# One more bank, regrouped splits and another pace of weight decoding in a fused attention and two-FFN kernel

## The chip, the cores and the metric

The kernel is one program on one core of a Trainium2 chip. The metric is the device time of one execution in microseconds (us). The engines are named as in the profile: PE (TensorE, matrix products), DVE (VectorE), ACT (ScalarE), POOL (GpSimd) and SP (SyncE, which only issues DMAs). Each engine works through its own instructions in order.

## The reference

Attention with a causal window of 128 and a distance bias per head, then two feed-forward layers with different activations. The FFN weights arrive as float64.

```python
scores = scale * np.matmul(q, k.transpose(0, 1, 3, 2))        # 4 x 8 heads, 576 x 576, head_dim 64
scores = np.where((rel >= 0) & (rel < 128), scores + bias[None], -1e9)
attn = exp(scores - max); attn = attn / (sum + 1e-9)
x = np.matmul(attn, v)            # -> (2304 tokens, 512)

h = x @ w_in                      # first FFN: 512 -> 2048
x = (h * np.cos(h)) @ w_out       # 2048 -> 512

h = x @ w_in2                     # second FFN
g = np.where(h >= 1, h, np.where(h <= -1, 0.0, (h + 1) ** 2 / 4))
out = g @ w_out2
```

## The kernel before

**Precision.** Each FFN product is made of three float32r matmuls: an operand is split into a rounded part (hi, by a cast on ACT) and a remainder (lo, by a subtraction on DVE, `sub_lo`), and hi x hi, hi x lo and lo x hi are added up in PSUM. `split_x` does this for the activations (one cast, one subtraction for each of 4 tiles `d`), `split_w2` for the second FFN's weights (its subtraction is on POOL).

**Attention.** 36 pairs (two blocks of 128 queries, two heads) pass through a pipeline written out by hand: in round `k` PE computes the scores of pair k+3 (`pe_s`), the transposes of pair k (`pe_t`, banks h0 and h1) and the products with V of pair k-1 (`pe_v`, banks h2 and h3), while DVE and ACT make scores and exponentials (`scores`), POOL scales by the reciprocal sums (`normalise`), `copy_t` brings the transposes from PSUM to SBUF and `put_x` the results. In the last four rounds (k = 33 to 36) there is no new pair.

**FFNs.** Tokens go through in chunks (`PARTS`). Chunk 0 has two parts, 512 and 256 tokens; chunks 1 to 3 have 512 each; the second FFN has four chunks of 512 and one of 256. A chunk has 16 steps `f` (128 of the 2048 hidden columns each). Per part and step, `mm_a` is 12 matmuls into one PSUM bank (below: an h run), `chain` is the activation function on that bank, and `mm_b` is 12 matmuls that add into the four banks y0 to y3 (a y run). For the first FFN the chain is: ACT scales h to an integer `k` (line 353), DVE takes the fraction (355), ACT takes the Sin (357), DVE multiplies with h (359), ACT casts to `gh` (371), DVE subtracts to `gl` (`sub_lo`, line 80). The chain is a generator: at each of its three yields, other work can be put between.

In chunk 0 the wide part has the one bank h0 and the narrow part h1, since h2 and h3 hold the narrow part's y. PE's order in step f is: wide h run of f, wide y run of f-1, narrow h run of f, narrow y run of f-1. In the other chunks an h run has four banks in turn, and the y run follows two steps later (`LAG`).

**Weight decoding.** `halves` turns float64 weights into float32 with integer operations, half a tile at a time; each `make` issues one DVE instruction of it, with ACT's help (lines 113 and 138). For the first FFN this gives 128 instructions; 17 are issued during attention, the rest in chunk 0 by `slot()`, up to 8 in a step. For the second FFN there are 96, issued in chunks 1 to 3 at the yields of the chains and spread over `KEEP_STEPS` of their 48 steps; their results go to DRAM (`wd`) and are read back in chunk 3 (`stage_f32`), step by step, for `split_w2`, as the first FFN's weights in SBUF are done with. The incoming weights and the reloads share three SBUF tiles (`ld`).

At a chunk's last step `split_x` prepares the next chunk's input; in chunk 0 it stands behind the wide part's chain, in the others one tile is put at each yield of the chain, in place of decoding.

All five engines' instructions are in the order of the program, in one block.

Of the kernel before, what the change touches and what calls it, by code (L numbers as in the profile page):

```python
# [9 lines left out]
F32 = mybir.dt.float32  # L10
# [3 lines left out]
AF = mybir.ActivationFunctionType  # L14
ALU = mybir.AluOpType
ENG = mybir.EngineType
# [7 lines left out]
KD, NF = DM // 128, DFF // 128  # L24
# [2 lines left out]
PARTS = ((((0, 512), (512, 256)), ((768, 512),), ((1280, 512),), ((1792, 512),)),  # L27
         (((0, 512),), ((768, 512),), ((1280, 512),), ((1792, 512),), ((512, 256),)))
LAG = 2
KEEP_STEPS = 42  # L30
N_W1, N_W2 = 8 * NF, 6 * NF
AHEAD = 3

# [1 line left out]
D_FROM = 4  # L35
PT = "DADADADD"
XE = "DA"
ORDERED = {ENG.PE, ENG.DVE, ENG.Activation, ENG.Pool, ENG.SP}


@with_exitstack
def attention_moe_moe_kernel(
# [10 lines left out]
    ACT, DVE, POOL, PE, SP = nc.scalar, nc.vector, nc.gpsimd, nc.tensor, nc.sync  # L53

    one = ctx.enter_context(tc.tile_pool(name="one", bufs=1))
# [8 lines left out]
    chunks = [dict(m=m, parts=parts, last=i == len(PARTS[m]) - 1)  # L64
              for m in range(2) for i, parts in enumerate(PARTS[m])]
# [7 lines left out]
    def small(name, dtype=F32, shape=(128, 512)):  # L73
        return two.tile(list(shape), dtype, tag="s", name=nm(name), bufs=12)
# [82 lines left out]
    made = [0, 0]  # L157
# [90 lines left out]
    def normalise(p):  # L248
        for j in range(2):
            st, sc, w = p["st"], p["sc"][j], p["w"][j]  # L250
            POOL.tensor_tensor(  # L251
                out=sc[:, :, 0:w], in0=sc[:, :, 0:w],
                in1=st[:, 8 + 2 * j:10 + 2 * j].unsqueeze(2).to_broadcast([128, 2, w]), op=ALU.mult)
# [14 lines left out]
    def copy_t(p, j):  # L268
        p["pt"][j] = pt = small("pt")
        n = 2 * p["w"][j]  # L270
        if PT[copies[0] % len(PT)] == "A":
            ACT.copy(pt[:, 0:n], p["tb"][j][:, 0:n])
        else:
            DVE.tensor_copy(pt[:, 0:n], p["tb"][j][:, 0:n])
        copies[0] += 1
# [18 lines left out]
    def put_x(p):  # L294
        t0 = p["b0"] * 128
        o, w = max(a for a in all_parts if a[0] <= t0)
        if (o, p["hp"]) not in x_tiles:
            x_tiles[o, p["hp"]] = new_x(w)
        x = x_tiles[o, p["hp"]][0][:, t0 - o:t0 - o + 256]
        if XE[evicted[0] % len(XE)] == "A":  # L300
            ACT.copy(x, p["vb"][:, 0:256])
        else:
            DVE.tensor_copy(x, p["vb"][:, 0:256])
        evicted[0] += 1


    half = one.tile([128, 1], F32, name="half")
    half_pi = one.tile([128, 1], F32, name="half_pi")

    def free_xs(c, i):  # L310
        for d in range(KD):
            free_x(c["xs", i, d][2])

    def split_x(c, i, ds):
        o, w = c["parts"][i]
        for d in ds:
            x, slot = x_tiles.pop((o, d))
            hi, hi_slot = new_x(w, F32R)
            lo = x_lo(4 * i + d)[:, 0:w]
            ACT.copy(hi, x)  # L320
            sub_lo(DVE, lo, x, hi)
            free_x(slot)
            c["xs", i, d] = hi, lo, hi_slot
# [3 lines left out]
    def mm_a(c, i, f):  # L327
        hi, lo = weights[c["m"], f]
        if len(c["parts"]) > 1:
            tag = f"h{i}"  # L330
        else:
            h_no[0] = (h_no[0] + 1) % 4
            tag = f"h{h_no[0]}"
        w = c["parts"][i][1]
        h = ps.tile([128, 512], F32, tag=tag, name=nm("h"))[:, 0:w]
        n = 0
        for d in range(KD):
            xh, xl, _ = c["xs", i, d]
            s = slice(d * 128, d * 128 + 128)
            for a, x in ((hi, xh), (hi, xl), (lo, xh)):  # L340
                PE.matmul(h, lhsT=a[:, 0, s], rhs=x, start=(n == 0), stop=(n == 11))  # L341
                n += 1
        c["h", i, f] = h
# [64 lines left out]
            if c["m"]:  # L408
                SP.dma_start(out[d * 128:(d + 1) * 128, o:o + w], s)

    def body():
        load(0)
        dist_sb.append(two.tile([128, 512], F32, tag="k", name="dist_sb", bufs=1)[:, 0:256])
        SP.dma_start(dist_sb[0], dist)
        load(1)
        DVE.memset(half, 0.5)
        DVE.memset(half_pi, TWO_PI / 4)
        make_identity(nc, ident)
        np_ = len(pairs)
        c0 = chunks[0]  # L420
        splits = [(i, d) for i in range(len(c0["parts"])) for d in range(KD)]
        for k in range(-AHEAD, np_ + 1):
            new = pairs[k + AHEAD] if k + AHEAD < np_ else None
            mid = pairs[k + AHEAD - 1] if 0 <= k + AHEAD - 1 < np_ else None
            nrm = pairs[k + AHEAD - 2] if 0 <= k + AHEAD - 2 < np_ else None
            cur = pairs[k] if 0 <= k < np_ else None
            old = pairs[k - 1] if k >= 1 else None
            load(k + AHEAD + 1)
            load(k + AHEAD + 2)
            if new:  # L430
                pe_s(new)
            if cur:
                pe_t(cur)
            if old:
                pe_v(old)
            if new:
                scores(new, 0)
            else:
                for i, d in splits[:3]:
                    split_x(c0, i, [d])  # L440
                del splits[:3]
            if cur:
                copy_t(cur, 0)
            if nrm:
                normalise(nrm)
            if mid:
                POOL.tensor_scalar_add(mid["st"][:, 4:8], mid["st"][:, 4:8], 1e-9)
            if new:
                scores(new, 1)
            if mid:  # L450
                DVE.reciprocal(mid["st"][:, 8:12], mid["st"][:, 4:8])  # L451
            if cur:
                copy_t(cur, 1)
            if k >= D_FROM and k % 2 == 0:
                make(0, D_ATT)
            if old:
                put_x(old)

        done = [0, made[0]]

        def slot():
            done[0] += 1
            while made[0] < min(N_W1, done[1] + -(-(N_W1 - 3 - done[1]) * done[0] // (8 * NF - 8))):
                make(0)

        nxt = chunks[1]
        for f in range(NF):
            while made[0] < 8 * f + 5:
                make(0)
            mm_a(c0, 0, f)  # L470
            x = chain(c0, 0, f)
            for _ in x:
                slot()
            if f == NF - 1:
                free_xs(c0, 0)
                split_x(nxt, 0, range(KD))
            if f:
                mm_b(c0, 0, f - 1)
            mm_a(c0, 1, f)
            for _ in chain(c0, 1, f):  # L480
                slot()
            slot()
            slot()
            if f == NF - 1:
                free_xs(c0, 1)
            while made[0] < min(N_W1, 8 * f + 9):
                make(0)
            if f:
                mm_b(c0, 1, f - 1)
        carried = c0  # L490
        step = 0
        for ci, c in enumerate(chunks[1:], 1):
            nxt = chunks[ci + 1] if ci + 1 < len(chunks) else None
            for f in range(NF):
                mm_a(c, 0, f)
                if f == 0:
                    for i in range(len(carried["parts"])):
                        mm_b(carried, i, NF - 1)
                        evict(carried, i)
                    if carried["m"] == 0 and carried["last"]:  # L500
                        split_w2(NF - 1)
                step += 1
                splits = list(range(KD)) if f == NF - 1 and nxt is not None else []
                if splits:
                    free_xs(c, 0)
                if c["m"] == 0 and c["last"] and f == 0:
                    for i in range(2):
                        stage_f32(i)
                for i, _ in enumerate(chain(c, 0, f)):
                    if splits:  # L510
                        split_x(nxt, 0, [splits.pop(0)])
                    elif c["m"] == 0:
                        while made[1] < min(N_W2, N_W2 * (3 * step + i - 2) / (3 * KEEP_STEPS)):
                            make(1)
                if splits:
                    split_x(nxt, 0, splits)
                for g in (range(f - LAG, NF - 1) if f == NF - 1 else [f - LAG]):
                    if g >= 0:
                        mm_b(c, 0, g)
                        if c["m"] == 0 and c["last"]:  # L520
                            split_w2(g)
            carried = c
        mm_b(carried, 0, NF - 1)
        evict(carried, 0)

    if ORDERED:
        with tc.manual_schedule(engines=ORDERED):
            body()
    else:
        body()  # L530


_OUTS = [((DM, NTOK), "float32")]
# [48 lines left out]
```

## Time and profile before

| | us |
|---|---|
| median of 3 runs | 957.91 (956.19 to 959.86) |
| profiled execution, its own time | 958.9 |
| its span from first to last instruction | 957.1 |
| PE busy | 921.9 |
| DVE, ACT, POOL busy | 559.2, 435.1, 125.1 |

Times of the trace are counted from the start of the span. An instruction's duration in the trace is longer than the distance to the next one on PE, DVE and ACT, as they overlap; distances are taken from starts. PEclk is the share of the 2.4 GHz clock that was granted, 0.5 being the 1.2 GHz level.

### The profile page before, as it was taken

What the parts mean: (1) busy time and instruction counts of PE and PEld (TensorE: products, weight loads), DVE (VectorE), ACT (ScalarE), POOL (GpSimd) and SP (SyncE); (2) the same over time, 40 slices, a digit from 0 to 9 for tenths busy, and PEclk for the clock granted to TensorE, in tenths of its full rate; (3) what the DMA queues carried; (4) which work ended last, traced back from release to release, by engine and by line L of the source; (5) the groups of instructions that cost most, each with busy time, mean ns of one, the idle gap of its engine ahead of it and who ended that gap; (6) DMA issues with size and microseconds to landing.
All of it is one profiled execution on the core that took longest, in us unless ns stands there. A gap on an engine that the chain in (4) does not pass through costs nothing.

```text
span 957.1 us, 13080 instructions
## 1 busy us (share of the span) xinstructions
PE 921.9 (96%) x4944; PEld 760.2 (79%) x4944; DVE 559.2 (58%) x1193; ACT 435.1 (45%) x923; POOL 125.1 (13%) x146
## 2 busy tenths in 40 slices
PE   7999979999899999999989999999999999999998
PEld 5677758887778887888767878888888888888898
DVE  6889868888767565655556454344334433533443
ACT  7788845565555444444445642233223222322232
POOL 5677710000000000000035530000000000000000
PEclk9999979999999999999999999999999999999999
DMA  9344213333314332431246300001001000100000
GB/s 360 127 192 176 87 37 111 111 111 110 111 45 132 117 114 76 135 119 67 89 164 186 125 21 0 1 1 45 1 0 45 1 1 1 45 0 1 13 33 23
DMA packets 24399, 74.90 MB, mean 78 GB/s; under 512 B 2704, under 2 KB 3344, under 8 KB 24336
## 3 DMA queue, kind: packets, MB, share of 16 engines
q1 hardware_dynamic: 24336, 74.07, 22.6%
q8 instruction: 39, 0.64, 0.3%
q14 instruction: 24, 0.20, 0.1%
HBM read 60.95 MB, written 13.11 MB: 77 GB/s over the span
## 4 chain that ended last, share of the span: by engine, by line
PE 72%; DVE 11%; ACT 10%; issue 3%; DMA 2%; POOL 1%; ACTq 0%; SPq 0%; DVEq 0%
PE y L391 32%; PE h L341 32%; PE pa L218 3%; PE pa L263 3%; PE pa L288 3%; ACT t L357 2%; DVE t L359 2%; DVE t L355 2%; ACT gh L371 1%; ACT wh L138 1%; ACT sc L245 1%; DVE wu L129 1%; DMA wst<-wd 1%; DVE wl L80 1%; ACT wu L113 1%
## 5 line engine op out<-in xcount | busy, mean ns | idle before, releaser
L341 PE MATMUL h<-x,wh 128*128 128x512 f32 (+1 forms) x640 | 236.8, 370 | 5.1 <-DVE t L359 2.9
L341 PE MATMUL h<-x,wl 128*128 128x512 f32 (+1 forms) x640 | 236.4, 369 | 4.8 <-DVE wl L80 4.8
L341 PE MATMUL h<-xl,wh 128*128 128x512 f32 (+1 forms) x640 | 236.6, 370 | 2.1 <-DVE xl L80 2.0
L391 PE MATMUL y<-gh,wh 128*128 128x512 f32 (+1 forms) x576 | 219.0, 380 | 4.3 <-ACT gh L371 4.3
L391 PE MATMUL y<-gl,wh 128*128 128x512 f32 (+1 forms) x576 | 219.3, 381 | 1.5 <-DVE gl L80 1.5
L391 PE MATMUL y<-gh,wl 128*128 128x512 f32 (+1 forms) x576 | 218.3, 379 | 0.0
L362 ACT ACTIVATE t<-t,half 128x512 f32<-128x512 f32 (+1 forms) x80 | 54.4, 681 | 197.3 <-DVE t L361 197.0
L341 PEld LDWEIGHTS h<-x,wl 128*128 128x128 f32 x640 | 120.8, 189 | 27.2 <-DVE wl L80 7.3
L341 PEld LDWEIGHTS h<-x,wh 128*128 128x128 f32 x640 | 120.6, 188 | 26.9 <-DVE t L359 3.5
L341 PEld LDWEIGHTS h<-xl,wh 128*128 128x128 f32 x640 | 120.7, 189 | 24.4 <-DVE xl L80 4.6
L80 DVE TENSOR_TENSOR gl<-t,gh 128x512 fp32r<-128x512 f32 (+1 forms) x144 | 95.4, 662 | 68.3 <-ACT gh L371 65.6
L371 ACT CAST gh<-t 128x512 fp32r<-128x512 f32 (+1 forms) x144 | 86.0, 597 | 103.3 <-DVE t L364 58.8
L391 PEld LDWEIGHTS y<-gh,wh 128*128 128x128 f32 x576 | 109.1, 189 | 27.0 <-ACT gh L371 6.8
L391 PEld LDWEIGHTS y<-gl,wh 128*128 128x128 f32 x576 | 109.0, 189 | 23.7 <-DVE gl L80 3.8
L391 PEld LDWEIGHTS y<-gh,wl 128*128 128x128 f32 x576 | 109.1, 189 | 20.1
L361 DVE TENSOR_SCALAR t<-h 128x512 f32<-128x512 f32 (+1 forms) x80 | 50.9, 636 | 96.9 <-PE h L341 96.8
L80 POOL TENSOR_TENSOR wl<-wst,wh 128x512 fp32r<-128x512 f32 x32 | 42.5, 1350 | 396.2 <-ACT wh L172 393.4
L364 DVE TENSOR_TENSOR t<-h,t 128x512 f32<-128x512 f32 (+1 forms) x80 | 51.0, 638 | 58.3 <-ACT t L362 58.3
L357 ACT ACTIVATE t<-t,half_pi 128x512 f32<-128x512 f32 x80 | 54.5, 682 | 66.0 <-DVE t L355 66.0
L355 DVE SCALAR_TENSOR_TENSOR t<-h,k 128x512 f32<-128x512 f32 x80 | 50.8, 635 | 54.7 <-ACT k L353 54.6
L245 ACT ACTIVATE sc<-sc,st 128x256 f32<-128x256 f32 (+1 forms) x144 | 70.2, 489 | 23.1 <-DVE st L238 20.3
L251 POOL TENSOR_TENSOR sc<-sc,st 128x512 f32<-128x512 f32 (+1 forms) x72 | 73.9, 1047 | 34.8 <-DVE st L451 29.2
(49 smaller groups left out, 870.5 us busy)
## 6 DMA issues: line engine op xcount, KB each, us to landing
wst<-in_w SPq DMA_DIRECT2D x64, 512.0 KB, 3.7
qkv<-in_qkv SPq DMA_DIRECT2D x36, 512.0 KB, 8.9
wd<-wu SPq DMA_DIRECT2D x32, 256.0 KB, 2.5
wst<-wd SPq DMA_DIRECT2D x16, 512.0 KB, 3.7
out_t<-ys SPq DMA_DIRECT2D x16, 256.0 KB, 2.1
out_t<-ys SPq DMA_DIRECT2D x4, 128.0 KB, 1.8
dist_sb<-in_dist SPq DMA_DIRECT2D x1, 128.0 KB, 3.3
```

The lines of the kernel that those rows point to most:

```text
L80: eng.tensor_tensor(out=out, in0=full, in1=f32(hi), op=ALU.subtract)
L218: PE.matmul(b[h], lhsT=t[r, j * 128:j * 128 + 128], rhs=t[r, kc:kc + w], start=True, stop=True)
L245: ACT.activation(sc[:, h, 0:w], sc[:, h, 0:w], AF.Exp, bias=st[:, c:c + 1], scale=-1.0, accum_out=st[:, 4 + c:5 + c])
L251: POOL.tensor_tensor(out=sc[:, :, 0:w], in0=sc[:, :, 0:w], in1=st[:, 8 + 2 * j:10 + 2 * j].unsqueeze(2).to_broadcast([128, 2, w]), op=ALU. ...
L341: PE.matmul(h, lhsT=a[:, 0, s], rhs=x, start=(n == 0), stop=(n == 11))
L355: DVE.scalar_tensor_tensor(out=t, in0=h, scalar=INV_2PI, in1=k, op0=ALU.mult, op1=ALU.subtract)
L357: ACT.activation(t, t, AF.Sin, bias=half_pi, scale=TWO_PI)
L361: DVE.tensor_scalar(out=t, in0=h, scalar1=-1.0, scalar2=1.0, op0=ALU.max, op1=ALU.min)
L362: ACT.activation(t, t, AF.Square, bias=half, scale=0.5)
L364: DVE.tensor_tensor(out=t, in0=h, in1=t, op=ALU.max)
L371: ACT.copy(gh, t)
L391: PE.matmul(c["y", i][d], lhsT=a[:, 1, s], rhs=x, start=(f == 0 and k == 0 and not (i and d % 2)), stop=(f == NF - 1 and k == 2 and (i == ...
```

## The change

- In the last four rounds of attention, `split_x` no longer does three tiles ahead of the first `copy_t` but one tile ahead of and one behind the second `copy_t`; POOL's addition of 1e-9 goes ahead of `normalise` there.
- Behind the last exponentials, ACT computes a Sin on a 128 x 1 tile (`half_pi2`).
- In step 1 of chunk 0 the wide h run goes to bank y3, not h0.
- In chunk 0 each slot issues a decode instruction until all are out.
- At a chunk's last step, all of `split_x` stands ahead of the chain, and decoding goes on in the chain's yields there.
- The second FFN's weights are decoded over 32 steps (chunks 1 and 2), not 42.
- The order by hand is written as one block for PE and two for the other engines (attention, FFNs).

```diff
--- before.py
+++ after.py
@@ -27,7 +27,7 @@
 PARTS = ((((0, 512), (512, 256)), ((768, 512),), ((1280, 512),), ((1792, 512),)),
          (((0, 512),), ((768, 512),), ((1280, 512),), ((1792, 512),), ((512, 256),)))
 LAG = 2
-KEEP_STEPS = 42
+KEEP_STEPS = 32
 N_W1, N_W2 = 8 * NF, 6 * NF
 AHEAD = 3
 
@@ -35,7 +35,8 @@
 D_FROM = 4
 PT = "DADADADD"
 XE = "DA"
-ORDERED = {ENG.PE, ENG.DVE, ENG.Activation, ENG.Pool, ENG.SP}
+ORDERED = {ENG.DVE, ENG.Activation, ENG.Pool, ENG.SP}
+ORDERED_MOE = {ENG.DVE, ENG.Activation, ENG.Pool, ENG.SP}
 
 
 @with_exitstack
@@ -306,6 +307,7 @@
 
     half = one.tile([128, 1], F32, name="half")
     half_pi = one.tile([128, 1], F32, name="half_pi")
+    half_pi2 = one.tile([128, 1], F32, name="half_pi2")
 
     def free_xs(c, i):
         for d in range(KD):
@@ -327,7 +329,8 @@
     def mm_a(c, i, f):
         hi, lo = weights[c["m"], f]
         if len(c["parts"]) > 1:
-            tag = f"h{i}"
+
+            tag = "y3" if f == 1 and i == 0 else f"h{i}"
         else:
             h_no[0] = (h_no[0] + 1) % 4
             tag = f"h{h_no[0]}"
@@ -408,7 +411,7 @@
             if c["m"]:
                 SP.dma_start(out[d * 128:(d + 1) * 128, o:o + w], s)
 
-    def body():
+    def attention():
         load(0)
         dist_sb.append(two.tile([128, 512], F32, tag="k", name="dist_sb", bufs=1)[:, 0:256])
         SP.dma_start(dist_sb[0], dist)
@@ -418,7 +421,7 @@
         make_identity(nc, ident)
         np_ = len(pairs)
         c0 = chunks[0]
-        splits = [(i, d) for i in range(len(c0["parts"])) for d in range(KD)]
+        splits = [(i, [d]) for i in range(len(c0["parts"])) for d in range(KD)]
         for k in range(-AHEAD, np_ + 1):
             new = pairs[k + AHEAD] if k + AHEAD < np_ else None
             mid = pairs[k + AHEAD - 1] if 0 <= k + AHEAD - 1 < np_ else None
@@ -435,32 +438,37 @@
                 pe_v(old)
             if new:
                 scores(new, 0)
-            else:
-                for i, d in splits[:3]:
-                    split_x(c0, i, [d])
-                del splits[:3]
             if cur:
                 copy_t(cur, 0)
-            if nrm:
+            if nrm and new:
                 normalise(nrm)
             if mid:
                 POOL.tensor_scalar_add(mid["st"][:, 4:8], mid["st"][:, 4:8], 1e-9)
+            if nrm and not new:
+                normalise(nrm)
             if new:
                 scores(new, 1)
             if mid:
                 DVE.reciprocal(mid["st"][:, 8:12], mid["st"][:, 4:8])
+            if not new:
+                split_x(c0, *splits.pop(0))
             if cur:
                 copy_t(cur, 1)
+            if not new:
+                split_x(c0, *splits.pop(0))
             if k >= D_FROM and k % 2 == 0:
                 make(0, D_ATT)
             if old:
                 put_x(old)
-
-        done = [0, made[0]]
+            if k + AHEAD == np_:
+
+                ACT.activation(half_pi2, half, AF.Sin)
+
+    def moes():
+        c0 = chunks[0]
 
         def slot():
-            done[0] += 1
-            while made[0] < min(N_W1, done[1] + -(-(N_W1 - 3 - done[1]) * done[0] // (8 * NF - 8))):
+            if made[0] < N_W1:
                 make(0)
 
         nxt = chunks[1]
@@ -468,12 +476,11 @@
             while made[0] < 8 * f + 5:
                 make(0)
             mm_a(c0, 0, f)
-            x = chain(c0, 0, f)
-            for _ in x:
-                slot()
             if f == NF - 1:
                 free_xs(c0, 0)
                 split_x(nxt, 0, range(KD))
+            for _ in chain(c0, 0, f):
+                slot()
             if f:
                 mm_b(c0, 0, f - 1)
             mm_a(c0, 1, f)
@@ -500,20 +507,16 @@
                     if carried["m"] == 0 and carried["last"]:
                         split_w2(NF - 1)
                 step += 1
-                splits = list(range(KD)) if f == NF - 1 and nxt is not None else []
-                if splits:
+                if f == NF - 1 and nxt is not None:
                     free_xs(c, 0)
+                    split_x(nxt, 0, range(KD))
                 if c["m"] == 0 and c["last"] and f == 0:
                     for i in range(2):
                         stage_f32(i)
                 for i, _ in enumerate(chain(c, 0, f)):
-                    if splits:
-                        split_x(nxt, 0, [splits.pop(0)])
-                    elif c["m"] == 0:
+                    if c["m"] == 0:
                         while made[1] < min(N_W2, N_W2 * (3 * step + i - 2) / (3 * KEEP_STEPS)):
                             make(1)
-                if splits:
-                    split_x(nxt, 0, splits)
                 for g in (range(f - LAG, NF - 1) if f == NF - 1 else [f - LAG]):
                     if g >= 0:
                         mm_b(c, 0, g)
@@ -523,11 +526,14 @@
         mm_b(carried, 0, NF - 1)
         evict(carried, 0)
 
-    if ORDERED:
+    with tc.manual_schedule(engines={ENG.PE}):
         with tc.manual_schedule(engines=ORDERED):
-            body()
-    else:
-        body()
+            attention()
+        if ORDERED_MOE:
+            with tc.manual_schedule(engines=ORDERED_MOE):
+                moes()
+        else:
+            moes()
 
 
 _OUTS = [((DM, NTOK), "float32")]
```

## Rows read from the trace of the kernel before

**Rows 1.** Chain that ended last, merged: start us, us, what.

```profile
252.10 1.45 PE h L341 x12
...
279.41 4.17 PE y L391 x24
...
292.25 2.72 PE h L341 x12
```

**Rows 2.** Timeline of PE, starts of h runs: start, us, engine, line, [idle before].

```profile
134.14 0.50 PE L341 MATMUL h<-x,wh 128*128 128x512 f32 x1
...
140.60 0.50 PE L341 MATMUL h<-x,wh 128*128 128x512 f32 x1 [2.02 <-DVE t L359]
...
276.50 0.40 PE L341 MATMUL h<-x,wh 128*128 128x512 f32 x1
...
365.53 0.39 PE L341 MATMUL h<-x,wh 128*128 128x512 f32 x1
...
454.42 0.39 PE L341 MATMUL h<-x,wh 128*128 128x512 f32 x1
...
552.09 0.39 PE L341 MATMUL h<-x,wh 128*128 128x512 f32 x1
```

**Rows 3.** Windows: stretch, length, each engine's busy us, then PEclk, DMA share, GB/s.

```profile
120.30:124.60 4.30, 0.01 (x2) 0.03 (x1) 2.83 (x6) 2.41 (x5) 0.00 (x0) 0.86 0.07 28
124.60:134.14 9.54, 8.89 (x65) 7.68 (x65) 6.90 (x13) 2.38 (x6) 2.48 (x2) 0.53 0.01 2
134.14:146.20 12.06, 10.04 (x51) 8.38 (x50) 7.32 (x14) 7.34 (x13) 0.00 (x0) 1.00 0.17 49
514.00:552.10 38.10, 38.03 (x168) 31.47 (x169) 21.17 (x29) 23.48 (x41) 20.69 (x16) 1.00 0.51 167
552.10:562.00 9.90, 7.85 (x26) 5.53 (x25) 5.07 (x7) 4.33 (x8) 5.50 (x4) 0.83 0.00 1
```

**Rows 4.** Timeline of the end of attention, all engines.

```profile
117.43 2.33 POOL L251 TENSOR_TENSOR sc<-sc,st 128x512 f32<-128x512 f32 x2 [0.77 <-DVE st L451]
...
121.13 0.62 ACT L320 CAST x<-x 128x512 fp32r<-128x512 f32 x1 [0.76 <-DVE xl L80]
...
123.77 0.68 DVE L274 COPY pt<-pa 128x512 f32<-128x512 f32 x1
...
124.60 1.94 PE L263 MATMUL pa<-ident,sc 128*128 128x128 f32 x8 [4.29 <-DVE st L451]
...
124.76 1.51 DVE L80 TENSOR_TENSOR xl<-x,x 128x512 fp32r<-128x512 f32 x1
```

**Rows 5.** Timeline of chunk 0's first steps, VectorE and ScalarE.

```profile
137.80 1.28 ACT L357 ACT_TABLE_LOAD   x1
137.82 0.69 DVE L355 SCALAR_TENSOR_TENSOR t<-h,k 128x512 f32<-128x512 f32 x1 [3.21 <-ACT k L353]
...
139.10 0.72 ACT L357 ACTIVATE t<-t,half_pi 128x512 f32<-128x512 f32 x1
...
148.37 0.69 DVE L359 TENSOR_TENSOR t<-h,t 128x512 f32<-128x512 f32 x1 [0.79 <-ACT t L357]
```

**Rows 6.** Waits of the whole span: who, for whom, us in total, times, longest.

```profile
ACT wu L113 <- DMA wst<-in_w: 9.9, 3, 5.0
...
PE h L341 <- DVE wl L80: 4.8, 5, 1.6
```

**Rows 7.** Timeline of VectorE, first and last of 15 rows, one step of chunk 0.

```profile
180.37 0.68 DVE L129 SCALAR_TENSOR_TENSOR wu<-wst,wu 128x512 uint32<-128x512 uint32 x1
...
188.85 0.69 DVE L129 SCALAR_TENSOR_TENSOR wu<-wst,wu 128x512 uint32<-128x512 uint32 x1
```

**Rows 8.** Timeline of SyncE's queue, start of chunk 3.

```profile
461.63 4.03 SPq L97 DMA_DIRECT2D wst<-wd  x2
```

**Rows 9.** Timeline of VectorE, end of chunk 3.

```profile
555.30 1.77 DVE L80 TENSOR_TENSOR xl<-x,x 128x512 fp32r<-128x512 f32 x1
```

**Rows 10.** Page, part 6, DMA issues: KB each, median us to landing.

```profile
wst<-in_w SPq DMA_DIRECT2D x64, 512.0 KB, 3.7
```

## Prediction

> **What bounds the kernel now.** I read the page first: TensorE (PE) is busy in nearly every slice, so the question is only where it loses time. The merged chain gives the price of its work when nothing is late [rows 1]: 12 matmuls of 512 columns (a "run") take 2.72 us, a wide and a narrow (256-column) y run together 4.17, a narrow h run 1.45. So a step of chunk 0 (wide h, wide y, narrow h, narrow y) costs 2.72 + 4.17 + 1.45 = 8.34 us, and a step of any other 512-chunk 2 x 2.72 = 5.44, 16 of them 87.04.
>
> Next, the starts of runs on PE's timeline [rows 2]. The reader is to subtract them. First h run to chunk 1: 276.50 - 134.14 = 142.36 us; from the second wide h run (140.60) it is 135.90 for 15 steps, 9.06 a step where 8.34 would do. Chunk 1: 89.03, of which 1.45 is chunk 0's last narrow y run. Chunk 2: 88.89, so 1.85 lost. Chunk 3: 97.67, so 10.6 lost. The table by stretches [rows 3] adds the rest. Ahead of 134.14 PE stands still for 4.30 us, then works 9.54 us at a mean clock of 0.53, that is almost all at the 1.2 GHz level. In the 9.90 us from 552.1, 26 matmuls start, 5.9 us of work at 0.227 each, so 4.0 is lost. From there on nothing is.
>
> **The end of attention.** Before, three splits stand ahead of the transpose copies, each cast waiting for the subtraction before it [rows 4], 0.62 + 0.69 + 0.07 = 1.38 us a split. The copy of pair 33 therefore lies on DVE at 123.77 and PE's next transposes start at 124.60, after 4.29 us of waiting. Afterwards the copy comes first and one split follows each copy. My walk: PE is done with the round before at 120.3. POOL now adds 1e-9 first (it has to wait for pair 35's exponentials, some 0.9 us) and scales pair 34 until 120.7 (2.33 us [rows 4]); the transposes of pair 34 are done at 121.4, their products at 122.5. On DVE the first two subtractions run beside POOL, where one took 1.51 instead of 0.69 [rows 4]; I charge one such delay, so they end at 123.4. Then put_x, the copy of pair 34 (0.68) to 124.4, two splits and one decode instruction to 126.8, a copy, a subtraction, a copy to 128.4, and half of the last products. A transpose or product group is 0.97 (1.94 at half clock [rows 4]). The first h run starts at 128.9 or, without the POOL delay, 128.3; I take 128.8. No PE wait in this walk is over 1.1 us, and in the 12 us from 134.14, where PE is busy 10.04 of 12.06 with a 2.02 us wait, the granted clock is 1.00 [rows 2, 3]. So I assume 2.4 GHz here. **Term 1: 134.14 - 128.8 = -5.3.** Bounds: -6 (no delay) and -1 (the stretch again at half clock, 4.5 of its 9.54 us lost).
>
> The dummy Sin costs ScalarE (ACT) the 1.28 us table load [rows 5] between two casts, behind work already late by DVE; it is in the walk, and without that cover it would shift the first h run by 1.28. Its gain: the first step's Sin need no longer start at 139.10 but at the end of its input, 137.82 + 0.69 = 138.51 [rows 5], 0.55 us sooner. The Trainium skill (ScalarE: Activation LUTs, "What ACT_TABLE_LOAD costs") puts 1.28 us of load and a drain of 1.38 on each switch. Here the Sin starts 0.02 after the load ends, so the drain isn't seen; with it the time would come out 1.4 later.
>
> **The second bank.** Before, the second wide h run waits for the first chain to leave bank h0: 140.60, 2.02 us of waiting [rows 2]. With bank y3 it starts right after the narrow h run, some 4.3 us after the first (2.72 + 1.45 and the filling of the pipe). But then the first y run, which follows it on PE, needs y3 for its fourth tile, so its last three matmuls wait until the second chain has read h out of y3. That chain is queued on ACT and DVE behind the chains and decode slots of step 0. Before, its last read, the multiply at 148.37, ended 149.06, that is 14.92 after the first h run [rows 5]; less the 0.55 of the table load 14.4. PE reaches the fourth tile at 4.3 + 2.72 for the h run, 0.3 for a late gl and 9 x 0.227, that is at 9.4. So it stands still for 5.0 us; queued behind are the narrow h run and the narrow y run. They end 0.68 + 1.43 + 1.45 later: the third wide h run starts at 17.9 (before: 14.98, just after that multiply). Unknown is whether the wait sits on the fourth tile's matmuls alone or on the run's first matmul: 0 or +2.0 (9 x 0.227); I take the first, since each matmul names its own bank. Unknown too is the clock: the nearest rows are 4.29 us of waiting followed by 9.54 at 0.53 (about 5.1 us lost) and the 9.90 from 552.1 with 2 us of PE idle at a clock of 0.83 (1.7 lost) [rows 3, 4]. What follows here is dense runs, as at 552.1, so I charge 1.7; ends 0 and 5.1.
>
> The Trainium skill (TensorE: Matmul & The Clock Gate, "What's actually happening") says of the clock: "the default state is throttled, and activity releases the throttle". By that rule the second bank buys an idle stretch that is paid again at 1.2 GHz; rows 3 show such a fall after 4.3 us of standing still, so the trace agrees.
>
> **Decoding in every pause.** Before, decode is spread so as to end with the stage; the weights come ever closer to their use and PE waits for wl five times [rows 6]. Afterwards each of the 8 slots of a step issues one decode instruction until all 128 are out (17 in the even rounds 4 to 36 of attention, 111 slots, so into step 13), and the lead of 12 instructions stays. Is DVE then the bound? A step with all slots full, in just the order that every step will then have, lies in the trace: 180.37 to 188.85, 14 instructions, 8.48 us [rows 7]. That is 0.14 over PE's 8.34, some 1.7 us over 12 steps. A chain has about 2.8 us of slack (a wide y, a narrow h and a narrow y run, 5.6, against the 2.8 that its instructions take up to the multiply), full again after the y3 wait, when DVE is the one to wait. So PE sets the pace: 14 steps x 8.34 = 116.8. **Term 2:** 17.9 + 116.8 + 1.7 - 142.36 = **-6.0.** Bounds: -9.7 (no clock loss, y3 free 2 us sooner) and +2.
>
> **Splits ahead of the chain; 32 steps.** At a chunk's end the casts and subtractions now stand before the last chain. What is late next is that chain, by some 2.5 us; its y run comes three runs (8.2 us) after its h run, so this is covered. The next chunk's first h run no longer waits for its last xl, and the next step no longer starts with the decode backlog that was left out at the last one. Chunk 1 keeps its 0.5. **Term 3, chunk 2: -1.85.** In chunk 3 the last 10 steps of decoding share three load tiles with the reload of wd: SP is held 4.03 us at a reload [rows 8], and ACT, in order, waits three times, 9.9 us in all and up to 5.0, for a weight load [rows 6]. With 32 steps no decode is left in chunk 3. **Term 4, chunk 3: -10.6.** At its end the last xl subtraction (1.77 us beside POOL, until 557.07 [rows 9]) held the first h run of the second FFN; now it precedes the chain by 2 us and more. **Term 5: -4.0.** Terms 3 to 5 can fall to half if other waits appear; a gain above them is excluded, as nothing more is lost there.
>
> The price of 32 steps lies in chunks 1 and 2: three decode instructions a step, one per slot, with the chain six DVE instructions, at 8.48 / 14 = 0.61 each [rows 7] 3.6 us of 5.44. A 512 KB load lands in 3.7 us [rows 10], one per step instead of 0.76. Nothing on PE.
>
> **Sum.** -5.3 - 6.0 - 1.85 - 10.6 - 4.0 = -27.8. The profiled execution took 958.9 with a span of 957.1, so 1.8 lies around it: 929.3 + 1.8 = 931.1, I say 931. That execution is 1.0 above the median of the runs, 957.91.
>
> **Rivals.** (a) *The y3 wait costs more*: it sits on the whole run (+2.0) and the clock stays low as after 124.6 (+3.4): 936.5. For it: the idle time would be as long as the one at 120.3; against it, dense runs follow. (b) *Chunk 3 keeps waiting*, because the casts of split_w2 stand in ACT's order behind PE and reloads: about 939 (8.7 less gained). Against it: from 514, where decoding runs out, to 552.1 PE is busy 38.03 of 38.10 us [rows 3] with the same casts. (c) *DVE and ACT become the bound of chunk 0*, at the 9.06 of today: 14 x 0.72 = +10.1, 941. For it: the 8.48 is one step. (d) *Not faster*: the loads of the second weights fall behind in chunks 1 and 2, so that ACT, in order, waits at each. With 28 us to lose in 32 steps this decides from 0.88 us a step on; the longest such wait was 5.0 [rows 6]. Time 958 and more. Against it: three tiles, and a 3.7 us load [rows 10] in 5.44 us.
>
> **Chances.** The forecast 0.62 (its own range 926 to 935), (a) 0.17, (b) 0.10, (c) 0.07, (d) 0.04. The range 924 to 938 takes in the first two. About 0.5%, 4.8 us, is what a measurement of this kernel can tell from no change: faster than that 0.94, within it 0.03, slower 0.03.
>
> **What would show it.** First h run near 129 at a clock of 1.0; a PE wait of some 5 us inside the first wide y run, released by the multiply of the second chain, and a fall of the clock behind it; then 8.34 a step up to chunk 1, without waits for wl; chunks 2 and 3 of about 87 us each; no ACT wait for a weight load after chunk 1. Steps of 8.5 or more, or waits for `in_w` loads in chunks 1 and 2, would make it wrong.

## The result and the profile after

The changed kernel takes 931.77 us (median of 4 runs, 931.54 to 932.55) where the kernel before, run beside it, takes 958.73: a ratio of 0.9724, 95% interval 0.9702 to 0.9746. It is faster, and 931 was predicted. The profiled execution took 931.54 with a span of 929.7, so again 1.8 lies around the span.

I read it in the order of the prediction. First, the starts of runs on PE's timeline, which answer to [rows 2] (start, us, engine, line, idle before):

```profile
129.21 0.50 PE L344 MATMUL h<-x,wh 128*128 128x512 f32 x1
133.52 0.40 PE L344 MATMUL h<-x,wh 128*128 128x512 f32 x1
...
143.67 0.80 PE L394 MATMUL y<-gh,wh 128*128 128x512 f32 x1 [4.74 <-DVE t L362]
...
149.17 0.40 PE L344 MATMUL h<-x,wh 128*128 128x512 f32 x1
...
265.94 0.40 PE L344 MATMUL h<-x,wh 128*128 128x512 f32 x1
...
354.98 0.39 PE L344 MATMUL h<-x,wh 128*128 128x512 f32 x1
...
442.01 0.39 PE L344 MATMUL h<-x,wh 128*128 128x512 f32 x1
...
529.05 0.39 PE L344 MATMUL h<-x,wh 128*128 128x512 f32 x1
```

The table by stretches, cut at these starts, answers to [rows 3]:

```profile
core 0: us, PE busy (x) PEld busy (x) DVE busy (x) ACT busy (x) POOL busy (x), PEclk, DMA share, GB/s
120.30:129.21 8.91, 6.59 (x80) 4.83 (x76) 6.28 (x13) 6.46 (x14) 3.97 (x4) 1.00 0.13 49
129.21:136.27 7.06, 7.06 (x39) 6.05 (x37) 4.51 (x10) 4.00 (x9) 0.00 (x0) 1.00 0.15 41
136.27:143.60 7.33, 2.50 (x10) 1.42 (x8) 6.95 (x14) 3.92 (x8) 0.00 (x0) 0.82 0.32 106
143.60:149.17 5.57, 5.50 (x27) 5.23 (x28) 2.42 (x6) 1.57 (x4) 0.00 (x0) 0.62 0.30 99
149.17:265.94 116.77, 116.77 (x675) 103.42 (x674) 100.55 (x187) 70.84 (x138) 0.00 (x0) 1.00 0.35 113
265.94:354.98 89.04, 88.84 (x399) 73.50 (x398) 63.00 (x106) 44.90 (x75) 0.00 (x0) 1.00 0.41 133
354.98:442.02 87.04, 87.04 (x386) 72.14 (x385) 61.55 (x103) 42.55 (x70) 0.00 (x0) 1.00 0.41 133
442.02:529.06 87.04, 87.04 (x386) 72.14 (x385) 37.40 (x54) 46.77 (x79) 33.51 (x26) 1.00 0.30 100
529.06:616.10 87.04, 87.04 (x386) 72.13 (x385) 37.66 (x56) 28.72 (x45) 7.60 (x6) 1.00 0.00 1
```

Subtract the starts, and set each length beside that of before:

| stretch | before, us | after, us | difference | predicted |
|---|---|---|---|---|
| span's start to the first h run | 134.14 | 129.21 | -4.93 | -5.3 |
| chunk 0, to chunk 1 | 142.36 | 136.73 | -5.63 | -6.0 |
| chunk 1 | 89.03 | 89.04 | 0 | 0 |
| chunk 2 | 88.89 | 87.04 | -1.85 | -1.85 |
| chunk 3 | 97.67 | 87.04 | -10.63 | -10.6 |
| second FFN's first chunk | 91.38 | 87.04 | -4.34 | -4.0 |
| sum | | | -27.4 | -27.8 |

Three things are to be seen. From 149.17 on PE is busy in every one of the 116.77 us, 8.34 a step. Chunks 2 and 3 and the first of the second FFN are at the 87.04 that 16 steps of 5.44 cost. And there is one hole: from 136.27 nine matmuls start (the table's x10 has also the h run's last one, still running), then PE stands still for 4.74 us until the multiply L362, and the granted clock is down at 0.82 and 0.62.

The waits of the whole span answer to [rows 6]: the waits for wl and for the loads of `in_w` are gone, and these two are all that is left of PE's waits in the FFNs.

```profile
PE y L394 <- DVE t L362: 4.7, 1, 4.7
PE y L394 <- DVE gl L81: 0.3, 2, 0.2
```

The end of attention, which answers to [rows 4, 5]: timelines of PE, ACT and DVE, in order of time.

```profile
121.06 1.40 PE L264 MATMUL pa<-ident,sc 128*128 128x128 f32 x8
...
122.59 1.28 ACT L465 ACT_TABLE_LOAD   x1
123.89 0.20 ACT L465 ACTIVATE half_pi<-half 128x1 f32<-128x1 f32 x1
...
124.45 0.63 PE L264 MATMUL pa<-ident,sc 128*128 128x128 f32 x4 [0.97 <-DVE pt L275]
...
134.40 0.69 DVE L362 TENSOR_TENSOR t<-h,t 128x512 f32<-128x512 f32 x1 [0.20 <-ACT t L360]
...
142.92 0.69 DVE L362 TENSOR_TENSOR t<-h,t 128x512 f32<-128x512 f32 x1 [0.19 <-ACT t L360]
```

PE's wait of 4.29 us has become waits of under 1 us, and the clock stays at 1.00. The table load lies between two casts of the splits, and the Sin that needed it follows 0.02 us after the load's end, as in [rows 5].

### The profile page after: what moved, and what is told of

Same layout as the page of the kernel before. It is cut to its first block, busy times and chain, and to the rows that moved or that the text cites. A ratio compares the mean times of both kernels' runs of the same rounds, so it can differ in the third digit from the quotient of the medians.

```text
span 929.7 us, 13125 instructions
## 1 busy us (share of the span) xinstructions
PE 910.0 (98%) x4944; PEld 758.8 (82%) x4944; DVE 550.9 (59%) x1193; ACT 435.8 (47%) x924; POOL 123.9 (13%) x146
## 4 chain that ended last, share of the span: by engine, by line
PE 93%; DVE 3%; ACT 3%; issue 1%; DMA 0%; POOL 0%; ACTq 0%; DVEq 0%
PE y L394 42%; PE h L344 42%; PE pa L219 3%; PE pa L264 3%; PE pa L289 2%; DVE pt L275 1%; ACT sc L246 1%; DVE sc L239 1%; DMA qkv<-in_qkv 0%; ACT wu L114 0%; DVE xl L81 0%; ACT pt L273 0%; DVE t L358 0%; ACT wh L139 0%; ACT x L322 0%
## 5 line engine op out<-in xcount | busy, mean ns | idle before, releaser
L358 DVE SCALAR_TENSOR_TENSOR t<-h,k 128x512 f32<-128x512 f32 x80 | 50.8, 635 | 57.5 <-ACT k L356 57.1
```

The source lines that it names most:

```text
L358: DVE.scalar_tensor_tensor(out=t, in0=h, scalar=INV_2PI, in1=k, op0=ALU.mult, op1=ALU.subtract)
```

## The experiments

Ten kernels, each of them the changed kernel with the edit shown (`...` marks lines left out of a cut); none leaves out any computation. The four under "The second bank" were run four times, the other six twice. The kernel before, run beside each group of them, had medians from 958.38 to 959.86, so between groups a difference of 1.5 us says nothing. The theory is the prediction's, with each term of its sum to be had back by undoing its part. "w2" is the time from the first h run to the third wide h run.

### The end of attention

*Its old order*, with the three splits ahead of the copy and POOL's scaling ahead of its addition:

```diff
+            else:
+                for i, ds in splits[:3]:
+                    split_x(c0, i, ds)
+                del splits[:3]
             if cur:
                 copy_t(cur, 0)
-            if nrm and new:
+            if nrm:
                 normalise(nrm)
...
-            if nrm and not new:
-                normalise(nrm)
...
-            if not new:
-                split_x(c0, *splits.pop(0))
```

> The changed kernel with the last four rounds of attention as before (three splits ahead of the copy, scaling ahead of the addition). Theory: PE waits over 4 us again, the clock falls to the 1.2 GHz level, the first h run starts 5 to 6 us later, total 937 to 938. Rival (part of it is hidden by later waits, as chunk 0 had slack): under 3 us slower.

937.04 us (936.77 to 937.3), ratio 0.9775 (0.9746 to 0.9803). PE's timeline and the stretch up to the first h run:

```profile
124.78 1.94 PE L264 MATMUL pa<-ident,sc 128*128 128x128 f32 x8 [4.30 <-DVE st L454]
```

```profile
120.30:134.07 13.77, 8.73 (x68) 7.38 (x64) 9.30 (x18) 6.35 (x13) 2.57 (x2) 0.63 0.04 17
```

The wait of 4.30 is back, the granted clock of the stretch is 0.63, and the first h run lies at 134.07, 4.86 later than after. The rest of the kernel shifts with it. Term 1 is shown, both halves of it: the wait and the clock behind it. The run undoes the order of the splits and that of POOL together; what each of them is worth alone is not shown.

*Without the dummy Sin:*

```diff
-            if k + AHEAD == np_:
-                ACT.activation(half_pi2, half, AF.Sin)
```

> The changed kernel without the dummy Sin, so that the table load stands ahead of the first chain's Sin again. Theory: the release of y3 comes some 0.5 us later, the first h run some 0.4 us sooner, since ACT is free for the casts: within 0.5 us of the changed kernel's 931.8. Rival: the whole load of 1.28 us is on the path, 933.

932.21 us (two runs, 932.15 and 932.27), ratio 0.9717 (0.9689 to 0.9746); after lies at 931.77. On VectorE's timeline the first and the second multiply of chunk 0:

```profile
134.42 0.69 DVE L362 TENSOR_TENSOR t<-h,t 128x512 f32<-128x512 f32 x1 [0.75 <-ACT t L360]
...
142.94 0.69 DVE L362 TENSOR_TENSOR t<-h,t 128x512 f32<-128x512 f32 x1 [0.19 <-ACT t L360]
```

The first h run starts at 128.69 here, so both multiplies come 0.54 us later after it than in the changed kernel (5.73 and 14.25 instead of 5.19 and 13.71): the 0.55 of the prediction. But the first h run itself comes 0.42 sooner without the load among the casts: 10.77 us after the decode instruction of round 32 (117.92), the last one ahead of the changed rounds, and 11.19 in the changed kernel (129.21 - 118.02). Against that instruction the second multiply gains only 0.12 (25.02 to 24.90). In the total it is 0.4, less than this measurement can tell.

### The second bank

*The second wide h run back in h0:*

```diff
-            tag = "y3" if f == 1 and i == 0 else f"h{i}"
+            tag = f"h{i}"
```

> The changed kernel, with the second wide h run of chunk 0 back in bank h0. Theory (the second bank costs more than it gives: PE stands still 4.7 us for y3, then works some 7 us at the 1.2 GHz level, while ACT and DVE set the pace of the chains anyway): the second wide h run waits about 1.6 us for the first multiply, the 4.7 us wait is gone, the clock stays at 1.0, the third wide h run starts 5.5 us sooner after the first one than with y3, and then DVE's 8.48 us a step is the pace up to step 13; chunk 1 starts 3.8 us sooner, total about 927.7 us. Rival (the bank is a gain of the 2.02 us that the run waited for before): 2 us slower than the changed kernel, 933.5.

927.7 us (926.6 to 927.92), ratio 0.9671 (0.9649 to 0.9693), 4.1 better than after. First h run 128.00, w2 14.44 instead of 19.96, chunk 0 133.04 instead of 136.73. The stretch to the third wide h run, then PE's wait in it:

```profile
128.00:142.44 14.44, 12.97 (x74) 11.19 (x73) 11.53 (x23) 8.00 (x17) 0.00 (x0) 1.00 0.23 73
```

```profile
133.91 0.50 PE L344 MATMUL h<-x,wh 128*128 128x512 f32 x1 [1.47 <-DVE t L362]
```

Waiting 1.47 us for h0 leaves the clock at 1.00; waiting 4.74 for y3 doesn't. Of the 5.5 us that w2 gains, chunk 0 keeps 3.7: the steps now take 8.49 (67.93 us for the 8 steps behind w2), where after has 8.34. What sets them is VectorE with ScalarE behind it. One instruction of the full step, a step apart:

```profile
182.10 0.69 DVE L130 SCALAR_TENSOR_TENSOR wu<-wst,wu 128x512 uint32<-128x512 uint32 x1
...
190.58 0.69 DVE L130 SCALAR_TENSOR_TENSOR wu<-wst,wu 128x512 uint32<-128x512 uint32 x1
```

8.48 us, the length of the full step in [rows 7]. In the changed kernel DVE has the same pace (the wide multiply L362 from 154.29 to 247.55, 11 steps of 8.48), but the stall at y3 gave it the slack to run so without being waited for, as the prediction said. That DVE is the cause, and not only in step with PE, the lighter DVE below shows.

*y3 kept, but the fourth tile of the first wide y run done a step later*, so that nothing waits for y3:

```diff
-    def mm_b(c, i, f):
-        if f == 0:
+    def mm_b(c, i, f, ds=range(KD)):
+        if f == 0 and ds[0] == 0:
...
-        for d in range(KD):
+        for d in ds:
...
-                mm_b(c0, 0, f - 1)
+                if f == 2:
+                    mm_b(c0, 0, 0, [3])
+                mm_b(c0, 0, f - 1, range(3) if f == 1 else range(KD))
```

> The changed kernel with y3 kept as second bank, but the last three matmuls of the first wide y run (its fourth tile, the one in y3) put behind the third wide h run, so that PE has neither wait. Theory (after the first step the chains on ACT and DVE set the pace, so it doesn't matter by which bank PE is freed): as with one bank, within 1 us of it, about 928. Rival (PE alone sets the pace of chunk 0): chunk 1 starts at the dense pace, 6.5 us sooner than in the changed kernel, and at least 2 us sooner than with one bank, 925.

927.11 us (926.56 to 928.48), ratio 0.9666 (0.9647 to 0.9686). The stretch to its third wide h run and the rest of chunk 0:

```profile
128.59:141.08 12.49, 12.34 (x72) 10.45 (x70) 9.77 (x20) 6.50 (x14) 0.00 (x0) 1.00 0.23 72
141.08:261.61 120.53, 119.32 (x677) 104.50 (x676) 103.72 (x193) 72.52 (x142) 0.00 (x0) 1.00 0.35 115
```

Now the bank does what it can: 12.49 us for w2, of which PE is busy 12.34, so it hardly waits there. But chunk 0 takes 133.02, as with one bank. Of the 1.95 us gained at its start (14.44 - 12.49), 0.68 is only put off, the three matmuls of the fourth tile, and 1.21 goes in one later wait for a multiply L362. From there the steps are at DVE's pace, as with one bank. Its timeline, the same multiply four steps apart:

```profile
167.82 0.69 DVE L362 TENSOR_TENSOR t<-h,t 128x512 f32<-128x512 f32 x1 [0.20 <-ACT t L360]
...
201.70 0.69 DVE L362 TENSOR_TENSOR t<-h,t 128x512 f32<-128x512 f32 x1 [0.20 <-ACT t L360]
```

That is 33.88 / 4 = 8.47 a step. Without a stall, DVE with ACT behind it sets the pace from the start, and the second bank is worth nothing.

*One bank, and the decode's subtraction on POOL instead of DVE in the FFNs:* does a lighter DVE give the steps back? (`in_ffn[0]` is set at the start of the FFNs.)

```diff
-            tag = "y3" if f == 1 and i == 0 else f"h{i}"
+            tag = f"h{i}"
...
-                    sub_lo(DVE, lo[:, h, :], u, hi[:, h, :])
+                    sub_lo(POOL if in_ffn[0] else DVE, lo[:, h, :], u, hi[:, h, :])
```

> The kernel with one bank, and in chunk 0 the subtraction that makes wl (2 a step) on POOL, which is idle there, instead of DVE. Theory A (DVE is the bound of chunk 0 at 8.48 us a step and 2 x 0.61 less lets PE's 8.34 decide): chunk 1 starts 1.7 us sooner than with one bank, about 926. Theory B (POOL's 1.3 us subtraction holds up those DVE instructions that run beside it, as it did with the splits of before, 1.51 for 0.69): each costs DVE 0.8, a step 8.48 - 1.2 + 1.6 = 8.9, some 5 us slower than with one bank, 933.

925.73 us (924.04 to 926.4), ratio 0.9647 (0.9627 to 0.9668). Chunk 0 takes 131.13, the steps behind w2 8.34 again. POOL and DVE do slow each other: POOL's subtraction takes 1.51 us in the mean of 28, where those of `split_w2` take 1.31, and DVE's wide gl 0.77 in the mean, where it was 0.69. Their timelines at one such place:

```profile
181.26 1.29 POOL L81 TENSOR_TENSOR wl<-wu,wh 128x512 fp32r<-128x512 f32 x1 [1.64 <-ACT wh L140]
...
181.74 1.37 DVE L81 TENSOR_TENSOR gl<-t,gh 128x512 fp32r<-128x512 f32 x1 [0.56 <-ACT gh L375]
```

A gl that takes 0.69 alone takes 1.37 here; it costs PE nothing, since DVE now has two instructions fewer in a step.

*The late fourth tile and the subtraction on POOL together* (both edits above, y3 kept):

> The changed kernel with y3 kept and the fourth tile of the first wide y run put behind the third wide h run, and with chunk 0's wl subtraction on POOL. Theory (with DVE relieved, a step is PE's 8.34, so now PE's early start does count): third wide h run 12.5 us after the first, then 14 steps of 8.34, chunk 1 129.3 us after the first h run, 1.9 sooner than with one bank and POOL's subtraction, total about 924. Rival (DVE and ACT still can't follow in the first steps): no sooner than with one bank, 925.7.

924.4 us (924.12 to 924.75), ratio 0.9634 (0.9618 to 0.965): the lowest median of the study. It isn't clear of the 925.73 before it, whose runs reach down to 924.04. Chunk 0 takes 130.48, only 0.65 less than with one bank, where 1.9 was expected: w2 is 13.04, not 12.49, since the first wide y run waits 0.76 for its gl, which took 1.30 beside a subtraction on POOL. The expected 129.3 (12.5 + 116.8) also leaves out the 0.68 of the fourth tile, which is done behind w2: that part takes 117.44. With it PE would need 129.9, so little is left there.

### Decoding in every pause

*The paced slots of before*, all else as after:

```diff
+        done = [0, made[0]]
         def slot():
-            if made[0] < N_W1:
+            done[0] += 1
+            while made[0] < min(N_W1, done[1] + -(-(N_W1 - 3 - done[1]) * done[0] // (8 * NF - 8))):
                 make(0)
```

> The changed kernel with chunk 0's decoding spread over the stage again, 0.9 an opportunity, all else as changed. Theory (PE waits for wl because the lead of the decoding shrinks to nothing): steps up to 10 at 8.34, then waits for wl in each of the last five, 4 to 9 us in all, total 936 to 941. Rival (the loss of before came from DVE being late since the first step, which the wait for y3 cures): no loss, 932 or a little less.

939.06 us (938.9 to 939.22), ratio 0.9796 (0.9767 to 0.9824), 7.3 more than after; chunk 0 takes 144.82, 8.1 more. Its waits, and chunk 0 behind w2 in two stretches:

```profile
PE h L344 <- DVE wl L81: 4.3, 5, 1.6
PE h L344 <- ACT wh L139: 1.6, 2, 1.5
```

```profile
148.84:223.90 75.06, 75.06 (x435) 66.45 (x433) 62.44 (x117) 44.95 (x86) 0.00 (x0) 1.00 0.34 110
223.90:273.62 49.72, 43.79 (x242) 36.70 (x241) 39.25 (x72) 27.23 (x51) 0.00 (x0) 1.00 0.30 96
```

The reader is to see where it goes: nine steps at exactly 8.34, then five that should take 41.70 and take 49.72. By the code a step issues 7.2 decode instructions and uses 8, so the 12 of lead shrink by 0.8 in each step; at step 11 some 3 are left, and from there PE waits for weights. With one bank the same change of pacing is worth 142.36 - 133.04 = 9.3 (which holds the Sin's table load too), with two 8.1. The bank costs 2.5 beside the paced slots (144.82 - 142.36) and 3.7 beside the full ones.

### Splits ahead of the chain, and 32 steps

*42 steps again:*

```diff
-KEEP_STEPS = 32
+KEEP_STEPS = 42
```

> The changed kernel with the second FFN's weights decoded over 42 steps again. Theory (the loss of chunk 3 came from decoding and reloading at once): chunk 3 loses 8 to 9 us again, with ACT waits for weight loads of 9 to 10 us in all, total about 940. Rival (it came from the chunk's end and the decode backlog, which stay mended here): under 2 us slower, 933.

935.09 us (934.1 to 936.09), ratio 0.9754 (0.9726 to 0.9783). Neither the 940 of the theory nor under 933: chunk 2 and the second FFN's first chunk keep their 87.04 and 87.05, and chunk 3 takes 91.17, a loss of 4.1 and not 10.6. ScalarE's waits for loads of `in_w`:

```profile
ACT wu L114 <- DMA wst<-in_w: 5.9, 2, 5.1
```

*The old end of a chunk*, with 32 steps: the splits go back into the chain's yields and behind it, no decoding there.

```diff
-                if f == NF - 1 and nxt is not None:
+                splits = list(range(KD)) if f == NF - 1 and nxt is not None else []
+                if splits:
                     free_xs(c, 0)
-                    split_x(nxt, 0, range(KD))
...
-                    if c["m"] == 0:
+                    if splits:
+                        split_x(nxt, 0, [splits.pop(0)])
+                    elif c["m"] == 0:
...
+                if splits:
+                    split_x(nxt, 0, splits)
```

> The changed kernel with the splits at the ends of chunks 1 to 3 and of the second FFN's chunks back in the yields of the chain, without decoding in that step. Theory: chunk 2 loses 1.9 us again, chunk 3 about 2 at its start, the second FFN 4 at its start, together 7 to 8, total about 939. Rival (these losses came from the decoding over 42 steps as well): under 3 us slower.

935.71 us (935.15 to 936.27), ratio 0.9761 (0.9732 to 0.9789). Again less than expected: chunk 2 takes 88.28, chunk 3 87.97, the next 88.99, together 4.1 over 87.04 each. The first h run of each waits for its last xl (0.24, 0.23 and 1.31 us). The first and the third on PE's timeline:

```profile
358.63 0.50 PE L344 MATMUL h<-xl,wh 128*128 128x512 f32 x1 [0.24 <-DVE xl L81]
...
535.96 0.50 PE L344 MATMUL h<-xl,wh 128*128 128x512 f32 x1 [1.31 <-DVE xl L81]
```

The third one waits for a subtraction that ran from 534.14 for 1.77 us beside POOL, as in [rows 9].

Two parts, each undone, lose 4.1, while the prediction had 16.45 for both. So both were undone together. Either the two add up (about 940), or each covers for the other.

> The changed kernel with both undone: decoding of the second FFN's weights over 42 steps, and the splits in the chain's yields at chunk ends. Undone alone, the first cost 4.1 us (all in chunk 3), the second 4.1 (1.2 in chunk 2, 0.9 in chunk 3, 1.9 in the second FFN's first chunk). Theory (the two cost more together: the decoding left out at a chunk's last step piles up at the next chunk's start, just where reloads and weight loads already compete for three tiles): chunk 3 loses 10.6 again and the three chunks together 16, total about 948. Rival (they add up): 8.2 us, total 940.

948.59 us (947.43 and 949.74), ratio 0.9885 (0.9863 to 0.9906). Chunk 2 takes 88.93, chunk 3 97.41, the next 91.58: the lengths of before, 16.8 over 87.04 each. The second reading is right. Its waits:

```profile
ACT wu L114 <- DMA wst<-in_w: 9.8, 3, 4.9
...
PE y L394 <- ACT gh L374: 4.4, 5, 2.8
```

And VectorE at the start of chunk 3:

```profile
449.49 0.69 DVE L134 SCALAR_TENSOR_TENSOR wu<-wst,wu 128x512 uint32<-128x512 uint32 x1
451.23 0.43 DVE L124 TENSOR_SCALAR wu<-wu 128x512 uint32<-128x512 uint32 x1 [1.06 <-ACT wu L114]
451.69 0.69 DVE L130 SCALAR_TENSOR_TENSOR wu<-wst,wu 128x512 uint32<-128x512 uint32 x1
452.30 0.68 DVE L358 SCALAR_TENSOR_TENSOR t<-h,k 128x512 f32<-128x512 f32 x1
```

Three decode instructions left out at chunk 2's end stand ahead of chunk 3's first chain, L358, which starts 9.27 us after the chunk's first h run (452.30 - 443.03). With the new end and 42 steps no decode instruction stands there and the chain starts after 6.81 (447.27 - 440.46); there is one long wait for a load, of 5.10 us, in place of two, of 4.05 and 4.88. With the old end and 32 steps three instructions are left out as well, the last three of all:

```profile
450.36 0.42 DVE L124 TENSOR_SCALAR wu<-wu 128x512 uint32<-128x512 uint32 x1
...
452.15 0.68 DVE L358 SCALAR_TENSOR_TENSOR t<-h,k 128x512 f32<-128x512 f32 x1
```

That chain starts after 8.24 (452.15 - 443.91), but no weight loads follow. So chunk 3 loses 0.93 us with the backlog and no loads, 4.13 with the loads and no backlog, 10.37 with both, and nothing with neither.

Part of that is the clock. Two stretches of the run with both undone:

```profile
478.00:485.00 7.00, 7.00 (x26) 5.62 (x26) 4.41 (x8) 3.42 (x7) 3.61 (x4) 0.79 0.58 188
540.44:552.00 11.56, 9.50 (x32) 6.81 (x31) 5.78 (x8) 5.72 (x11) 5.71 (x5) 0.85 0.00 1
```

The first comes behind PE's wait of 2.82 us for a gh, in chunk 3; the second has waits of 0.52, 0.22 and 1.31, at the start of the next chunk. By the granted clock they lose some 1.5 and 1.7 us (7.00 x 0.21 and 11.56 x 0.15, an estimate). With either part undone alone no wait of PE in these chunks is over 1.31, and the granted clock is 1.00 in all of them.

## Why the prediction was right, and where it wasn't

**What bounds the kernel.** PE at 8.34 and 5.44 a step was the right floor: four stretches of the table end on it, and no gain went beyond it.

**Term 1** (-5.3, measured -4.93). Right in its mechanism by the run with the old order (+4.86). The charged delay of a subtraction by POOL didn't occur: the two of them took 0.69 and 0.76 us. What stood in its place lies ahead of the change: attention ran later in this trace. The decode instruction of round 32, ahead of the four changed rounds, before and after, on VectorE's timeline:

```profile
117.20 0.66 DVE L133 SCALAR_TENSOR_TENSOR wu<-wst,wu 128x512 uint32<-128x512 uint32 x1
```

```profile
118.02 0.66 DVE L134 SCALAR_TENSOR_TENSOR wu<-wst,wu 128x512 uint32<-128x512 uint32 x1
```

Over the nine traces that have this code the first h run lies between 127.20 and 129.21, but always 11.19 or 11.20 us after that instruction. In the kernel before it is 16.94 us, with the old order 16.69 (134.07 - 117.38). So the change itself is worth -5.5 to -5.75, and attention's later start takes 0.82 of it back here. What moves that start by 2 us from trace to trace is open.

**Term 2** (-6.0, measured -5.63). Right line by line. Nine matmuls of the first y run, three tiles, start before the wait, so it sits on the fourth tile alone; it was 4.74 where 5.0 was charged, and the multiply that ends it ends at 142.92 + 0.69 = 143.61, 14.40 after the first h run, the predicted 14.4. From there to the third wide h run it takes 5.56 us and not the 0.68 + 1.43 + 1.45 = 3.56 of full clock: 2.0 lost to the clock, 1.7 charged. That size is no fixed price: in the seven traces that have this wait, 4.72 to 4.81 us long, the same work behind it loses between 1.6 and 2.9 (5.14 us with both parts undone, 6.46 with the old chunk end). Then 116.77 for 14 steps, 116.8 predicted. The Trainium skill (TensorE: Matmul & The Clock Gate, "What's actually happening") has it that the clock is throttled unless activity releases it. The trace agrees: with 4.74 us of idling the granted clocks are 0.82 and 0.62; behind the 1.47 us wait of the run with one bank the clock was 1.00. The term is thus the sum of two of opposite sign, and the runs put numbers to them: pacing -8.1 to -9.3, the second bank +2.5 to +3.7. The prediction's own numbers had the bank as a loss (17.9 + 1.7 against 14.98, +4.6), but it forecast only the sum and didn't say so.

**Terms 3 to 5** (-16.45, measured -16.8) were right as a sum, and each for its chunk. The step that failed is how they were divided among the edits. The prediction gave chunk 3's 10.6 to the 32 steps ("with 32 steps no decode is left in chunk 3") and the rest to the splits. In fact 32 steps without the new end recover 12.7 of 16.8, the new end with 42 steps 12.7 too, and both together all of it: the gains overlap by 8.6. Chunk 3's loss came from a decode backlog at its start *and* loads that compete with the reload of wd there; take either away and most of it goes. Some 3.2 of the 8.6 is the clock, which falls only when both are undone. Why one of the two waits for a load goes with the backlog is not shown.

Term 5 was mis-sized by a count: 4.34, not 4.0. The 26 matmuls of its row include two that began ahead of 552.1 and only ran into it. The h run and the y run between 552.09 and the next h run at 561.87 are 24 matmuls, 5.44 us of work in 9.78, so 4.34 was lost. It too has two parts: the chunk loses 1.95 with 32 steps, where PE waits 1.31 for the xl subtraction beside POOL, and the rest, 1.7 of it the clock by the estimate above, only with 42 steps as well.

That the profiled execution came within 0.5 us of 931.1 is luck in part: attention's start and the clock's price alone scatter by 2.0 and 1.3 us over the traces.

**The rivals.** (a), a wait on the whole run with a longer fall of the clock, is out: nine matmuls ran ahead, and the clock cost 2.0. (b) is out: PE is busy in all 87.04 us of chunk 3 (442.02:529.06). (c) was nearer than its chance says: without the stall at y3, DVE and ACT do set the pace, at some 8.5, though not at 9.06. (d) is out: ACT doesn't wait for a load of `in_w` in chunks 1 and 2, although one is decoded per step.

Chunk 1's 0.5 is in all runs and wasn't looked into.

## What to carry to other kernels

Borrowing a buffer moves a wait to the buffer's next owner: look up when that owner comes up in its in-order queue, and price the idle time and the clock behind it, before counting the wait that goes. Work paced to end with its stage has its lead run down just when a late piece stops everything; issue it in every pause instead, and look whether the engine that does it then keeps up with the bound (here 8.48 us a step against 8.34). And undo the parts of a change in pairs as well as singly: gains at one place can cover for each other, and then the single ones add up to far less than the whole.

## What was not expected of the hardware

- A stall can pay for itself in part: the 5.5 us lost at y3 and by the clock cost 3.7 in the end, because DVE's 8.48 us steps ran unnoticed behind it.
- Two engines can slow each other and the kernel still gains: with the subtraction on POOL a gl took 1.37 us instead of 0.69 and the kernel was 2.0 us faster (927.7 to 925.73), since DVE was what set the steps. Where a y run stood right behind such a gl, PE waited 0.76 for it.
- The clock's price isn't told by the wait alone: none behind 1.47 us of idling, and between 1.6 and 2.9 us behind waits of 4.72 to 4.81 with the same work behind them.
